# An adaLN transformer block on one core: reordered loads, layer norm and projections around the chunk boundaries

## The chip, the cores and the metric

One core of a Trainium2 chip (trn2) runs the whole program. The metric is device time in microseconds. The kernel before took 952.77 us in the median of five runs (951.03 to 953.43).

## What is computed

A block of 2048 tokens and width 1024, in bf16. Six modulation vectors come from one condition vector; linear attention with 32 heads of 32 is followed by a gated feed-forward network (FFN) of width 3584.

```python
mod = (silu(c) @ w_mod).reshape(1, 6, 1, -1)
sa, ca, ga, sb, cb, gb = (mod[:, i] for i in range(6))
h = layernorm(x) * (1 + ca) + sa
q, k, v = split_heads(h @ wqkv)
pq, pk = phi(q), phi(k)            # phi(t) = where(t > 0, t + 1, exp(t)) + 1e-6
o = (pq @ (pk^T v)) / (pq . sum(pk) + 1e-6)
x = x + ga * (merge_heads(o) @ wo)
h = layernorm(x) * (1 + cb) + sb
x = x + gb * ((gelu(h @ w_gate) * (h @ w_up)) @ w_down)
```

## The kernel before

The program is one list of operations in Python order. A recorder (`T.op`, `T.mm`, `T.dma`) puts each operation into the queue of its engine and adds the semaphore waits that its operands need; so the order in the source is the order on every engine, and an instruction that waits holds up all that stands behind it on the same engine. All matmuls are recorded at L209 and most DMAs at L197. In SBUF one arena is divided by hand, and buffers that lie over each other make waits.

Tokens go in 16 tiles of 128, and in 4 chunks of 512.

*K/V stage.* Four 1 MB panels of w_mod give the vectors ca and sa (`modT_vec`). Then each tile passes the stages of `ln_stages` in a software pipeline (`run_pipeline`): statistics on VectorE, a power on GpSimd (L445), the normalised tile on ScalarE (L451), a DMA transpose on the SP queue (L454), the modulation by eight 128x128 instructions on GpSimd (L460). `kv_groups` multiplies the tile by the panels in the order k0, v0, k1, v1. The four panel loads are one hook (`kv_panel_loads`), ahead of the first transpose on SP.

*Attention.* A loop over `p` takes pairs of tiles: q products, the chain on VectorE that gives the scaled features (`chain_pair`, from `d_prod` at L594 to `d_pqs` at L616), their transposes on SP (L623), the numerator of a chunk (`numT`, evicted by ScalarE at L631), and half an output projection (`wo_proj`, evicted at L644) from a queue. `wo_proj` also issues the loads of the x tiles of the next chunk on GpSimd's queue.

*FFN.* For each chunk, seven pairs of gate and up panels (1 MB each) pass through four panel slots; each pair gives 64 matmuls of 512 columns (448 a chunk), and the GELU runs on ScalarE (L738, L739, L743) and VectorE (L740, L741, L746, the last step of a chunk at L750). Then 224 matmuls make the down projection of the chunk's four tiles; VectorE scales and adds (L771, L775) and GpSimd's queue issues the store.

The input of the FFN, hT2, is made by the second layer norm. For chunk 0 its first six stages are recorded at `p == npairs`, its transposes and modulations behind all output projections. For the later chunks the six stages stand ahead of the down projection, and the transpose and the modulation of tile jj are recorded behind the store of tile jj (`pendingF`). hT2 lies over the last part of oT, which the output projections read. The normalised tiles of chunk 0, hn2a, lie where the first part of the down weights goes.

## Time and profile before

| | us |
|---|---|
| median of five runs | 952.77 |
| lowest, highest | 951.03, 953.43 |
| profiled execution, its own time | 950.31 |
| span of the profiled execution | 948.5 |
| TensorE (PE) busy in it | 854.5 |
| VectorE (DVE) | 442.4 |
| ScalarE (ACT) | 336.7 |
| GpSimd (POOL) | 166.5 |

The profile is of one execution. A busy time is the sum of an engine's instructions; it is an average over stages, so a hole of TensorE has to be read at its place: which wait ended it. Matmul instructions overlap and some of their records can be missing, so counts of matmuls in a stretch can be a few low. PE stands for the matmuls, PEld for their weight loads, SPq for the SP engine's queue of DMA issues.

### The profile page before, as it was taken

The page shows a single profiled execution, that of the slowest core. Times are in us where ns is not written, and L with a number is a line of the kernel's source. Part 1 is how long each engine was busy: PE and PEld are TensorE (multiplying, and loading weights), DVE is VectorE, ACT ScalarE, POOL GpSimd, SP SyncE. Part 2 cuts the span into 40 slices and gives each one's busy share as a digit, 9 for nine tenths or more (in the row PEclk, how much of TensorE's full clock was granted, in tenths as well). Part 3 has the DMA queues.
Part 4 walks back from the last instruction along what each step waited for, and adds up shares of the span by engine and source line. Part 5 has one row for each costly group of instructions (what it writes and reads, how often), then busy time and mean ns, then how long its engine had stood idle before and what let it go on. Part 6 is the DMA issues. An engine that isn't in the chain of part 4 may idle for free.

```text
span 948.5 us, 11061 instructions
## 1 busy us (share of the span) xinstructions
PE 854.5 (90%) x4193; PEld 389.2 (41%) x4193; DVE 442.4 (47%) x890; ACT 336.7 (36%) x572; POOL 166.5 (18%) x352
## 2 busy tenths in 40 slices
PE   1399999999977499989979998979999897999898
PEld 1144445544432144434434443434444343444343
DVE  5165431399873155563135556115555412555411
ACT  1244431465545154441025444004455201544300
POOL 3596632000011400002310000330000231000000
PEclk9999999999997699999989999989999998999999
DMA  9755208334322956707014521702541530534000
GB/s 328 193 150 161 41 16 275 125 67 78 71 53 55 296 178 225 264 3 221 34 40 150 178 88 27 218 23 89 178 138 41 126 130 11 178 125 142 1 23 22
DMA packets 131189, 112.91 MB, mean 119 GB/s; under 512 B 52801, under 2 KB 122433, under 8 KB 131137
## 3 DMA queue, kind: packets, MB, share of 16 engines
q1 hardware_dynamic: 125104, 91.24, 33.3%
q0 software_dynamic: 6016, 20.98, 6.5%
q8 instruction: 33, 0.54, 0.2%
q14 instruction: 20, 0.16, 0.1%
q10 hardware_dynamic: 16, 0.00, 0.0%
HBM read 95.42 MB, written 4.19 MB: 105 GB/s over the span
## 4 chain that ended last, share of the span: by engine, by line
PE 84%; issue 6%; DVE 3%; DMA 2%; ACT 2%; POOL 2%; SPq 0%; POOLq 0%; ACTq 0%; DVEq 0%
PE ps L209 84%; DMA arena<-in_w_mod_dram 2%; POOL arena L460 1%; DVE arena L599 0%; DVE arena L616 0%; ACT arena L631 0%; DVE arena L589 0%; ACT arena L451 0%; DMA arena<-arena 0%; DVE arena L771 0%; ACT arena L644 0%; DVE arena L750 0%; DVE arena L775 0%; ACT arena L739 0%; DVE arena L594 0%
## 5 line engine op out<-in xcount | busy, mean ns | idle before, releaser
L209 PE MATMUL ps<-arena 128*128 128x512 bf16 (+2 forms) x4192 | 854.4, 365 | 83.1 <-POOL arena L460 31.1
L209 PEld LDWEIGHTS ps<-arena 128*128 128x128 bf16 x4192 | 389.1, 99 | 548.0 <-issue 72.0
L738 ACT ACTIVATE arena<-ps 128x512 bf16<-128x512 f32 x112 | 66.9, 597 | 227.6 <-PE ps L209 227.6
L741 DVE SCALAR_TENSOR_TENSOR arena<-ps,arena 128x512 bf16<-128x512 f32 x112 | 77.5, 692 | 120.4 <-ACT arena L739 120.4
L460 POOL TENSOR_SCALAR arena<-arena 128x128 bf16<-128x128 bf16 x256 | 113.9, 456 | 50.1 <-DMA arena<-arena 49.2
L740 DVE SCALAR_TENSOR_TENSOR arena<-arena,ps 128x512 bf16<-128x512 bf16 x112 | 77.1, 688 | 93.0 <-ACT arena L738 93.0
L739 ACT ACTIVATE arena<-ps 128x512 bf16<-128x512 f32 x112 | 66.9, 597 | 130.6 <-PE ps L209 130.6
L771 DVE TENSOR_TENSOR arena<-ps,arena 128x512 bf16<-128x512 f32 x32 | 22.1, 692 | 146.6 <-PE ps L209 146.6
L445 POOL TENSOR_TENSOR arena<-arena 128x1 f32<-128x1 f32 x32 | 18.0, 568 | 344.8 <-DVE arena L442 344.8
L746 DVE SCALAR_TENSOR_TENSOR arena<-arena 128x512 bf16<-128x512 bf16 x108 | 73.6, 682 | 0.0
L743 ACT ACTIVATE arena<-arena 128x512 bf16<-128x512 bf16 x112 | 69.6, 622 | 0.0
L197 POOL DMA_DIRECT2D out_dram<-arena x16 | 9.3, 584 | 245.5 <-DVE arena L775 245.5
L451 ACT ACTIVATE arena<-arena 128x1024 bf16<-128x1024 bf16 x32 | 38.0, 1233 | 27.2 <-DVE arena L448 27.2
L197 POOL DMA_DIRECT2D arena<-in_A_x_dram x32 | 17.9, 562 | 115.5 <-DVE arena L647 77.1
L644 ACT ACTIVATE arena<-ps 128x512 bf16<-128x512 f32 x32 | 18.7, 595 | 33.7 <-PE ps L209 33.7
L578 ACT ACTIVATE arena<-ps 128x512 bf16<-128x512 f32 x32 | 19.5, 609 | 19.4 <-PE ps L209 11.3
L647 DVE TENSOR_TENSOR arena<-arena 128x512 bf16<-128x512 bf16 x32 | 13.2, 424 | 27.0 <-ACT arena L644 26.8
L496 ACT ACTIVATE arena<-ps 128x512 bf16<-128x512 f32 x16 | 9.6, 598 | 37.9 <-PE ps L209 37.9
L494 ACT ACTIVATE arena<-ps 128x512 bf16<-128x512 f32 x16 | 9.6, 598 | 37.7 <-PE ps L209 37.7
L436 DVE BATCH_NORM_STATS2 arena<-arena 128x6 f32<-128x512 bf16 x32 | 21.6, 675 | 0.0
L435 DVE BATCH_NORM_STATS2 arena<-arena 128x6 f32<-128x512 bf16 x32 | 20.7, 647 | 0.0
L579 ACT ACTIVATE arena<-ps 128x512 bf16<-128x512 f32 x32 | 19.5, 608 | 0.0
(49 smaller groups left out, 218.5 us busy)
## 6 DMA issues: line engine op xcount, KB each, us to landing
arena<-in_B_w_gate_dram SPq DMA_DIRECT2D x28, 1024.0 KB, 5.3
arena<-in_B_w_up_dram SPq DMA_DIRECT2D x28, 1024.0 KB, 7.3
arena<-in_A_x_dram POOLq DMA_DIRECT2D x32, 256.0 KB, 3.2
arena<-in_w_mod_dram POOLq DMA_DIRECT2D x8, 1024.0 KB, 12.1
arena<-in_B_w_down_dram SPq DMA_DIRECT2D x7, 1024.0 KB, 9.6
arena<-in_A_wqkv_dram SPq DMA_DIRECT2D x6, 1024.0 KB, 12.4
arena<-in_w_mod_dram SPq DMA_DIRECT2D x4, 1024.0 KB, 14.2
out_dram<-arena POOLq DMA_DIRECT2D x16, 256.0 KB, 2.3
```

The costliest lines, as they stand in the source:

```text
L197: return self.op(eng, lambda e: e.dma_start(out_ap, in_ap), R=R, W=W, ctr=ctr, inc=16)
L209: ins = t.matmul(o, l, r, start=(fs and i == 0), stop=(ls and i == n - 1))
L436: T.op("dve", lambda v: v.bn_stats(st[:, 6:12], x_ap[:, 512:1024]), R=[x_ap], W=[st[:, 6:12]])
L451: T.op("act", lambda a: a.activation(hn, x_ap, AF.Identity, bias=nm, scale=rs), R=[x_ap, nm, rs], W=[hn])
L460: T.op("pool", lambda g, blk=blk, t=t: g.tensor_scalar(blk, blk, c1T[:, t:t + 1], sT[:, t:t + 1], ALU.mult, ALU.add), R=[blk, c1T, sT], W= ...
L738: T.op("act", lambda a, sqz=sqz, bg=bg: a.activation(sqz, bank(bg), AF.Square, scale=math.sqrt(GELU_A)), R=[bank(bg)], W=[sqz])
L739: T.op("act", lambda a, usb=usb, bu=bu: a.activation(usb, bank(bu), AF.Copy), R=[bank(bu)], W=[usb])
L740: T.op("dve", lambda v, sqz=sqz, bg=bg: v.scalar_tensor_tensor(sqz, sqz, 1.0, bank(bg), ALU.add, ALU.mult), R=[sqz, bank(bg)], W=[sqz])
L741: T.op("dve", lambda v, dstA=dstA, usb=usb, bg=bg: v.scalar_tensor_tensor(dstA, bank(bg), 0.5, usb, ALU.mult, ALU.mult), R=[bank(bg), usb] ...
L743: T.op("act", lambda a, th=th, sqz=sqz: a.activation(th, sqz, AF.Tanh, scale=GELU_C), R=[sqz], W=[th])
L746: T.op("dve", lambda v, pd=pd, pth=pth: v.scalar_tensor_tensor(pd, pth, 1.0, pd, ALU.add, ALU.mult), R=[pth, pd], W=[pd])
L771: T.op("dve", lambda v, dst=dst, b=b, cols=cols: v.tensor_tensor(dst, bank(b), modGB[:, cols], ALU.mult), R=[bank(b), modGB[:, cols]], W=[ ...
```

## The change

1. The K/V panels are loaded in two hooks: k0 and v0 first, k1 and v1 at step 6 of the pipeline, which is behind the first transpose. The slots follow the order k0, v0, k1, v1.
2. `modT_vec` gets a parameter to hand back its eviction instead of issuing it. Both calls leave it off, so the order there is the old one. `load_panel` and `wd_part` get a parameter for the queue, which nobody uses.
3. Chunk 0's second layer norm writes a buffer of its own, hT2a, at 8 KB of the arena, where only the broadcast vector bc of the K/V stage had been. The chain of the last pair of tiles moves into `p == 7`. In `p == 7` the output projection stands behind the transposes and the numerator, and numerator 2 so ahead of half of projection 1. The layer norm's first five stages are recorded at `p == 8`, the normalising on ScalarE between the last tiles of projection 2, then the transposes; tiles 0 and 1 are modulated on GpSimd, tiles 2 and 3 on ScalarE between the tiles of projection 3.
4. The first gate and up panels are loaded at `p == 8`, ahead of the transposes of tiles 14 and 15. The first panel of chunk 0 is a call of its own (`gateup_panel`, the old loop body). The first part of the down weights is loaded at panel 2.
5. For the later chunks, the whole layer norm with transposes and modulations is recorded ahead of the down projection and its stores.
6. The first down product of a chunk is two groups of matmuls on the same bank, 26 and 2 of the 28 tiles of AT, each with its own waits.

```diff
-    def load_panel(src_ap):
+    def load_panel(src_ap, eng="sp"):
...
-        T.dma("sp", panel[k], src_ap, d_panel[k])
+        T.dma(eng, panel[k], src_ap, d_panel[k])
...
+    hT2a = view(8 * KB, [P, 4, NDT, P], BF16)
...
+    ks0, vs0, ks1, vs1 = [(panel_use[0] + i_) % NPANEL for i_ in range(4)]
 
     def kv_panel_loads():
-        a = [load_panel(wqkv_v[:, :, n * 512:(n + 1) * 512]) for n in (2, 3, 4, 5)]
-        assert tuple(a) == (ks0, ks1, vs0, vs1)
+        a = [load_panel(wqkv_v[:, :, n * 512:(n + 1) * 512]) for n in (2, 4)]
+        assert a == [ks0, vs0]
+
+    def kv_panel_loads_2():
+        a = [load_panel(wqkv_v[:, :, n * 512:(n + 1) * 512]) for n in (3, 5)]
+        assert a == [ks1, vs1]
...
     add_hook(1, kv_panel_loads)
+    add_hook(6, kv_panel_loads_2)
...
+    def ln2_0_items():
+        return [ln_stages(x1[:, jj, :], cb1T, sbT, hT2a[:, jj, :, :], d_trh[jj], hn2a_t, mod_eng=("pool" if jj < 2 else "act")) for jj in range(4)]
...
-        if 1 <= p <= npairs:
+        if 1 <= p < npairs:
             chain_pair(2 * (p - 1), 2 * (p - 1) + 1)
         if er_a is not None:
             q_minadd(er_a)
             q_minadd(er_b)
             q_ttadd(er_a)
             q_ttadd(er_b)
-        if wo_queue:
+            if p == npairs - 1:
+                chain_pair(2 * p, 2 * p + 1)
+        if p == npairs:
+            its0 = ln2_0_items()
+            run_pipeline([st_[:5] for st_ in its0])
+        if p < 7 and wo_queue:
             q_, jjs = wo_queue.pop(0)
             wo_proj(q_, jjs)
...
+        if 7 <= p <= npairs and wo_queue:
+            q_, jjs = wo_queue.pop(0)
+            wo_proj(q_, jjs)
         if p == npairs:
-            ln2_0_build()
-            run_pipeline([st_[:6] for st_ in ln2_0_items])
-    while wo_queue:
-        q_, jjs = wo_queue.pop(0)
-        wo_proj(q_, jjs)
-    for st_ in ln2_0_items:
-        st_[6]()
-    for st_ in ln2_0_items:
-        st_[7]()
+            kg0 = load_panel(wg_v[:, :, 0:512])
+            ku0 = load_panel(wu_v[:, :, 0:512])
+        if p == npairs + 1:
+            wo_queue.pop(0)
+            wo_proj(2, (2,))
+            its0[0][5]()
+            its0[1][5]()
+            wo_proj(2, (3,))
+            its0[2][5]()
+            its0[3][5]()
+            for st_ in its0:
+                st_[6]()
+            its0[0][7]()
+            its0[1][7]()
+    wo_proj(3, (0, 1))
+    its0[2][7]()
+    wo_proj(3, (2,))
+    its0[3][7]()
+    wo_proj(3, (3,))
...
+    gateup_panel(0, 0, hT2a, kg0, ku0)
     for q in range(NSC):
-        prevA = None
+        hT2c = hT2a if q == 0 else hT2
         for n in range(NFP):
+            if q == 0 and n == 0:
+                continue
...
+            if q == 0 and n == 2:
+                wd_part(0)
...
         if q + 1 < NSC:
-            nxt = ln2_items(q + 1)
-            run_pipeline([st_[:6] for st_ in nxt])
-            pendingF = [(st_[6], st_[7]) for st_ in nxt]
-        else:
-            pendingF = []
+            run_pipeline(ln2_items(q + 1))
...
-                T.mm(its)
+                if jj == 0 and dc == 0:
+                    T.mm(its[:26], last_stop=False)
+                    T.mm(its[26:], first_start=False)
+                else:
+                    T.mm(its)
...
-            if pendingF:
-                ftr, fmod = pendingF.pop(0)
-                ftr()
-                fmod()
```

Three places show how the instructions now stand; lines of the changed kernel have other numbers. First SP's queue at the start of the program, as a piece of the difference (all buffers lie in the arena; a transpose of L454 is L458 in the changed kernel):

```order
 L197 DMA arena<-in_w_mod_dram 128x8x512 x4
-L197 DMA arena<-in_A_wqkv_dram 128x8x512 x4
-L454 DMA_TRANSPOSE arena<-arena 128x8x128 x16
+L197 DMA arena<-in_A_wqkv_dram 128x8x512 x2
+L458 DMA_TRANSPOSE arena<-arena 128x8x128
+L197 DMA arena<-in_A_wqkv_dram 128x8x512 x2
+L458 DMA_TRANSPOSE arena<-arena 128x8x128 x15
```

The first transpose stands behind two panel loads instead of four, the others behind four loads and the first transpose.

Second ScalarE's queue at the end of the attention part, from the last q product to the first instruction of the FFN. Before (L631 evicts a numerator, L644 an output projection, L451 normalises, L738 is the FFN):

```order
L579 ACTIVATE arena<-ps 128x512
L644 ACTIVATE arena<-ps 128x512 x4
L631 ACTIVATE arena<-ps 128x512 x8
L644 ACTIVATE arena<-ps 128x512 x4
L451 ACTIVATE arena<-arena 128x1024 x4
L644 ACTIVATE arena<-ps 128x512 x4
L631 ACTIVATE arena<-ps 128x512 x8
L644 ACTIVATE arena<-ps 128x512 x8
L738 ACTIVATE arena<-ps 128x512
```

The same stretch of ScalarE's queue in the changed kernel (L636 for L631, L649 for L644, L455 for L451, L688 for L738, and L467 modulates):

```order
L584 ACTIVATE arena<-ps 128x512
L636 ACTIVATE arena<-ps 128x512 x8
L649 ACTIVATE arena<-ps 128x512 x8
L636 ACTIVATE arena<-ps 128x512 x8
L649 ACTIVATE arena<-ps 128x512 x2
L455 ACTIVATE arena<-arena 128x1024 x2
L649 ACTIVATE arena<-ps 128x512 x2
L455 ACTIVATE arena<-arena 128x1024 x2
L649 ACTIVATE arena<-ps 128x512 x4
L467 ACTIVATE arena<-arena 128x128 x8
L649 ACTIVATE arena<-ps 128x512 x2
L467 ACTIVATE arena<-arena 128x128 x8
```

Numerator 2 moved ahead of half of projection 1, the normalising went from ahead of projection 2's second half and numerator 3 to between its last two tiles, and two modulations of eight instructions came in between the tiles of projection 3.

Third GpSimd's queue at the boundary from chunk 0 to chunk 1 of the FFN, before (L445 is the power of the layer norm, L460 the modulation):

```order
L445 TENSOR_TENSOR arena<-arena 128x1 x4
L197 DMA out_dram<-arena 128x1024
L460 TENSOR_SCALAR arena<-arena 128x128 x8
L197 DMA out_dram<-arena 128x1024
L460 TENSOR_SCALAR arena<-arena 128x128 x8
L197 DMA out_dram<-arena 128x1024
L460 TENSOR_SCALAR arena<-arena 128x128 x8
L197 DMA out_dram<-arena 128x1024
L460 TENSOR_SCALAR arena<-arena 128x128 x8
```

The same boundary of GpSimd's queue in the changed kernel (L449 for L445, L464 for L460):

```order
L449 TENSOR_TENSOR arena<-arena 128x1 x4
L464 TENSOR_SCALAR arena<-arena 128x128 x32
L197 DMA out_dram<-arena 128x1024 x4
```

All four modulations stand ahead of the four stores.

## Rows read from the trace of the kernel before

**Rows 1.** Page, part 1: busy us (share of the span) and instructions of each engine.

```profile
PE 854.5 (90%) x4193; PEld 389.2 (41%) x4193; DVE 442.4 (47%) x890; ACT 336.7 (36%) x572; POOL 166.5 (18%) x352
```

**Rows 2.** Waits of PE: line, awaited engine: us in total, times, longest.

```profile
PE ps L209 <- POOL arena L460: 31.1, 2, 17.2
PE ps L209 <- issue: 18.5, 3, 6.4
PE ps L209 <- DVE arena L750: 10.5, 4, 2.6
```

**Rows 3.** Timeline, PE, 255 to 345: start, us, instructions, idle before and releaser.

```profile
254.78 10.09 PE L209 MATMUL ps<-arena 128*128 128x512 bf16 x46
267.75 14.85 PE L209 MATMUL ps<-arena 128*128 128x512 bf16 x68 [2.88 <-ACT arena L631]
287.23 2.06 PE L209 MATMUL ps<-arena 128*128 128x512 bf16 x4 [4.63 <-ACT arena L644]
292.58 16.28 PE L209 MATMUL ps<-arena 128*128 128x512 bf16 x64 [3.29 <-ACT arena L631]
322.73 22.59 PE L209 MATMUL ps<-arena 128*128 128x512 bf16 x92 [13.87 <-POOL arena L460]
```

**Rows 4.** Windows: us, busy us of PE, PEld, DVE, ACT, POOL, PEclk, DMA share, GB/s.

```profile
322.73:328.00 5.27, 5.27 (x13) 1.87 (x14) 0.69 (x1) 0.60 (x1) 0.00 (x0) 0.50 1.09 353
479.64:482.00 2.36, 2.36 (x6) 0.84 (x7) 0.00 (x0) 0.00 (x0) 0.00 (x0) 0.50 0.00 0
550.00:570.00 20.00, 20.00 (x94) 9.11 (x93) 11.15 (x17) 10.08 (x18) 0.00 (x0) 1.00 0.33 106
```

**Rows 5.** Chain that ended last, in order of time: start, us, work; FFN stages.

```profile
322.73 99.44 PE ps L209 x448
...
424.77 48.53 PE ps L209 x224
...
793.20 99.72 PE ps L209 x448
```

**Rows 6.** Timeline, DVE: first and last step of the chain of tiles 14 and 15.

```profile
264.82 1.29 DVE L594 TENSOR_TENSOR arena<-arena 128x1024 bf16<-128x1024 bf16 x2
...
269.18 2.35 DVE L616 TENSOR_TENSOR arena<-arena 128x1024 bf16<-128x1024 bf16 x2
```

**Rows 7.** DMA issues: queue, count, KB each, median us to landing (whole span; 18 to 40).

```profile
arena<-in_B_w_up_dram SPq DMA_DIRECT2D x28, 1024.0 KB, 7.3
...
arena<-in_A_wqkv_dram SPq DMA_DIRECT2D x2, 1024.0 KB, 12.7
```

**Rows 8.** Lines of ACT, forms apart: count, busy us, mean ns, idle before.

```profile
L451 ACT ACTIVATE arena<-arena 128x1024 bf16<-128x1024 bf16 x32 | 38.0, 1233 | 27.2 <-DVE arena L448 27.2
...
L644 ACT ACTIVATE arena<-ps 128x512 bf16<-128x512 f32 x32 | 18.7, 595 | 33.7 <-PE ps L209 33.7
...
L404 ACT ACTIVATE arena<-ps 128x8 f32<-128x8 f32 x2 | 0.4, 178 | 23.8 <-PE ps L209 23.8
```

**Rows 9.** Timeline, boundary from chunk 0 to 1: transposes, last store, last modulation.

```profile
431.44 5.39 SPq L454 DMA_TRANSPOSE arena<-arena  x4
...
475.24 0.59 POOL L197 DMA_DIRECT2D out_dram<-arena  x1 [8.00 <-DVE arena L775]
475.88 3.44 POOL L460 TENSOR_SCALAR arena<-arena 128x128 bf16<-128x128 bf16 x8
```

**Rows 10.** Timeline and chain, K/V start; a load, the first transpose, what follows.

```profile
15.42 4.87 SPq L197 DMA_DIRECT2D arena<-in_A_wqkv_dram  x2
...
24.52 6.48 SPq L454 DMA_TRANSPOSE arena<-arena  x1
...
35.05 3.44 POOL L460 TENSOR_SCALAR arena<-arena 128x128 bf16<-128x128 bf16 x8 [11.19 <-DMA arena<-arena]
...
38.60 134.41 PE ps L209 x824
...
48.72 0.60 ACT L494 ACTIVATE arena<-ps 128x512 bf16<-128x512 f32 x1 [1.24 <-PE ps L209]
```

More of the change, by code (lines that the diff above doesn't have):

```diff
@@ L394, in _build, with modT_vec @@
     T.op("pool", lambda g: g.iota(vm.rearrange("p (a b) -> p a b", a=4), [[DH, 4], [0, DH]], base=0, channel_multiplier=-1), W=[vm])
-    def modT_vec(pan_lo, pan_hi, dstT, plus1, b):
+    def modT_vec(pan_lo, pan_hi, dstT, plus1, b, defer=False):
         for t in range(NDT):
@@ L403, in modT_vec @@
         if plus1:
-            T.op("act", lambda a: a.activation(dstT, src, AF.Identity, bias=1.0, scale=1.0), R=[src], W=[dstT])
+            ev = lambda: T.op("act", lambda a: a.activation(dstT, src, AF.Identity, bias=1.0, scale=1.0), R=[src], W=[dstT])
         else:
-            T.op("act", lambda a: a.activation(dstT, src, AF.Copy), R=[src], W=[dstT])
-    modT_vec(panel[pan_ca0], panel[pan_ca1], ca1T, True, next_bank())
-    modT_vec(panel[pan_sa0], panel[pan_sa1], saT, False, next_bank())
+            ev = lambda: T.op("act", lambda a: a.activation(dstT, src, AF.Copy), R=[src], W=[dstT])
+        if defer:
+            return ev
+        ev()
+    early_mod_evacs = [modT_vec(panel[pan_ca0], panel[pan_ca1], ca1T, True, next_bank()),
+                       modT_vec(panel[pan_sa0], panel[pan_sa1], saT, False, next_bank())]
     T.op("dve", lambda v: v.tensor_scalar(t1m, vm, 0.0, None, ALU.is_le), R=[vm], W=[t1m])
@@ L660, in chain_pair, with gateup_panel, gelu_flush @@
                 f(t_)
-    ln2_0_items = []
-    def ln2_0_build():
-        for jj in range(4):
-            ln2_0_items.append(ln_stages(x1[:, jj, :], cb1T, sbT, hT2[:, jj, :, :], d_trh[jj], hn2a_t))
+    def ln2_0_items():
+        return [ln_stages(x1[:, jj, :], cb1T, sbT, hT2a[:, jj, :, :], d_trh[jj], hn2a_t, mod_eng=("pool" if jj < 2 else "act")) for jj in range(4)]
+    gelu_cnt = [0]
+    gelu_state = {"prevA": None}
+    def gateup_panel(q, n, hT2c, kg, ku):
+        for j4 in range(4):
+            jf = n * 4 + j4
+            kk = gelu_cnt[0]
+            gelu_cnt[0] += 1
+            bg = next_bank()
+            bu = next_bank()
+            items_g = [(bank(bg), panel[kg][:, t, j4 * P:(j4 + 1) * P], hT2c[:, :, t, :]) for t in range(NDT)]
+            items_u = [(bank(bu), panel[ku][:, t, j4 * P:(j4 + 1) * P], hT2c[:, :, t, :]) for t in range(NDT)]
+            T.mm(items_g)
+            T.mm(items_u)
+            sqz = sqz_t[kk % NGT]
+            th = th_t[kk % NGT]
+            usb = usb_t[kk % NGT]
+            dstA = AT[:, jf, :]
+            T.op("act", lambda a, sqz=sqz, bg=bg: a.activation(sqz, bank(bg), AF.Square, scale=math.sqrt(GELU_A)), R=[bank(bg)], W=[sqz])
+            T.op("act", lambda a, usb=usb, bu=bu: a.activation(usb, bank(bu), AF.Copy), R=[bank(bu)], W=[usb])
+            T.op("dve", lambda v, sqz=sqz, bg=bg: v.scalar_tensor_tensor(sqz, sqz, 1.0, bank(bg), ALU.add, ALU.mult), R=[sqz, bank(bg)], W=[sqz])
+            T.op("dve", lambda v, dstA=dstA, usb=usb, bg=bg: v.scalar_tensor_tensor(dstA, bank(bg), 0.5, usb, ALU.mult, ALU.mult),
+                 R=[bank(bg), usb], W=[dstA])
+            T.op("act", lambda a, th=th, sqz=sqz: a.activation(th, sqz, AF.Tanh, scale=GELU_C), R=[sqz], W=[th])
+            if gelu_state["prevA"] is not None:
+                pd, pth = gelu_state["prevA"]
+                T.op("dve", lambda v, pd=pd, pth=pth: v.scalar_tensor_tensor(pd, pth, 1.0, pd, ALU.add, ALU.mult),
+                     R=[pth, pd], W=[pd])
+            gelu_state["prevA"] = (dstA, th)
+    def gelu_flush():
+        if gelu_state["prevA"] is not None:
+            pd, pth = gelu_state["prevA"]
+            T.op("dve", lambda v, pd=pd, pth=pth: v.scalar_tensor_tensor(pd, pth, 1.0, pd, ALU.add, ALU.mult), R=[pth, pd], W=[pd])
+            gelu_state["prevA"] = None
     npairs = NST // 2
@@ L723, in _build @@
                 wd_part(n)
[L724 to L757 removed]
+            if q == 0 and n == 2:
+                wd_part(0)
+            gateup_panel(q, n, hT2c, kg, ku)
+        gelu_flush()
+        if q + 1 < NSC:
+            run_pipeline(ln2_items(q + 1))
         for jj in range(4):
@@ L777, in _build @@
             T.dma("pool", out2d[j * P:(j + 1) * P, :], stg, d_o[so % NXR])
-            if pendingF:
-                ftr, fmod = pendingF.pop(0)
-                ftr()
-                fmod()
-        while pendingF:
-            ftr, fmod = pendingF.pop(0)
-            ftr()
-            fmod()
     for k in range(NXR):
```

38 lines of the change are left out of this document (2 added, 36 removed).

## The prediction

> **What bounds the kernel now.** I began with the page's busy line: TensorE is busy for 854.5 of 948.5 us, 90%, and no other engine is near that [rows 1]. So the kernel is a chain of matmuls with holes, and the questions are which work ends each hole late and what the matmuls just behind a hole cost. The list of TensorE's waits names the big holes [rows 2]: two on the GpSimd line that applies the modulation (31.1 us, 17.2 and 13.9), three of some 6.2 us put down to "issue" (18.5 us), four on the last GELU step on VectorE (10.5 us). The timeline of TensorE around the end of the attention part [rows 3] shows four more close together: 2.88, 4.63, 3.29 and 13.87 us. The windows [rows 4] show what follows a long hole: from 322.73 and from 479.64 the granted clock is 0.50, the 1.2 GHz level, with matmuls half as fast, while in the middle of a panel it is 1.00, the 2.4 GHz level. After the 2.6 us hole ahead of the down projection nothing is lost: 224 matmuls in 48.53 us are 216.6 ns each [rows 5]. I use that as the full-speed price of one 512-column matmul.
>
> **The change part by part.**
>
> *Second layer norm of the first chunk (chunk 0).* Before, its transposes write hT2, which lies over the tail of oT, so they wait until the last output projection has read oT; then come three tiles of modulation on GpSimd, and only then the first gate matmul, at 322.73. The numerator product of chunk 2 ends at 254.78 + 10.09 = 264.87 [rows 3]. From there to 322.73 there are 136 matmuls, 29.5 us at 216.6 ns: without holes or half speed the gate would start at 294.3. The difference, 28.4 us, is what can be had; in it are the holes 2.88 + 4.63 + 3.29 + 13.87 = 24.7 and the slow pieces of [rows 3] (64 matmuls in 16.28 us where 13.9 would do). The new order leaves the same number of matmuls: numerator 2 moves ahead of 32 of them (half of output projection 1).
>
> Is everything else ready by 294.3? I lay the new order on that clock, counting back: output projection 3 takes 6.93 + 3.47 + 3.47, so its parts end at 287.4, 290.8 and 294.3; projection 2's last two tiles end at 277.0 and 280.5; numerator 3 starts at 271.8.
> (a) The attention chain of tiles 14 and 15 on VectorE ran from 264.82 to 271.53, 6.7 us [rows 6]. It now stands ahead of half of projection 1 and starts some 5 us earlier, near 260, so its two transposes are issued by 267. On SP they stand behind two new 1 MB panel loads; these may start when the last q product has run, near 257, and a load of that kind lands 7.3 us after its issue [rows 7], so they are out of the way by 266. The transposes land about 270, 2 us before numerator 3 needs them. This is the tightest place on SP.
> (b) ScalarE normalises tiles 0 and 1 behind the eviction that ends at 277.6, at 1.23 us each [rows 8], then tiles 2 and 3 behind the one at 281.1; the last transpose is issued near 283.6 and lands by 287. GpSimd modulates tiles 0 and 1 in 2 x 3.45 us [rows 9] after its last x load, near 284 to 291: in time.
> (c) Tiles 2 and 3 are now modulated on ScalarE, 8 instructions of 128x128 each, which the trace does not show. The nearest rows are 178 ns for 8 columns and 595 ns for 512 [rows 8]; by columns between them 128 columns take 0.28 us, so a tile 2.2 us. Tile 2: 288.0 to 290.2; the two evictions of the next projection tile to 291.9; tile 3 to 294.1. Just in time: stall 0. At 0.18 us it is earlier still; at 0.60 us a tile is 4.8 us, tile 3 ends near 298.7, and the stall is 4.4 us. I take 0, the value by columns.
> The Trainium skill's page "ScalarE: Activation LUTs", section "What ACT_TABLE_LOAD costs", speaks against this part: it gives an instruction a fixed cost, and more for each per-partition scale or bias, of which these have both. By its figures I estimate 0.39 us each, back to back; tile 3 would end near 295.3 and the gate would wait 1.0 us, so the sum would be 1.0 us smaller. No run here shows it yet.
> (d) TensorE hands eight banks to ScalarE at numerator 2 and again at 3: I allow 0.5 us. Term: 28.4 - 0.5 = **27.9 us**, from 22 (the 4.4 us stall, and a short slow restart) to 28.4.
> (e) The first gate and up panels are loaded early. The second pair needs the slots of the output weights, free only at 294.3; 7.3 us to landing and a load in front of it make some 9 to 10 us, and the first panel's 64 matmuls cover 13.9. Cost nothing; without that cover, up to 3 us. The first down weights move two panels later, with 27 us of matmuls in front.
>
> *Chunk boundaries.* After each of the first three down projections, the last output store waits on GpSimd for VectorE, and the last tile's modulation stands behind it in the queue: 475.24, then 475.88 for 3.44 us [rows 9], and the gate starts at 479.64. Now all four modulations stand ahead of the stores. The transposes are issued between 431.44 and 436.8 [rows 9], so four times 3.45 us end near 452, with 21 us of down projection left; the stores, which nobody waits for but the ring, start some 10 us later. The hole goes, three times. Term: **18.5 us** [rows 2], bounded by 3 x 6.4 = 19.2.
>
> *Split of the first down product.* It read all 28 tiles of AT at its first matmul and so waited for the last GELU step. Now the first 26 wait for nothing late: 26 x 0.2166 = 5.6 us of cover for a tail of 2.6 us. Term: **10.5 us** over four chunks [rows 2].
>
> *Clock.* The gate/up stages take 99.44 to 99.72 us for 448 matmuls [rows 5], where 448 x 0.2166 = 97.05: 2.4 to 2.7 us each, and [rows 4] put that into the first 5 us behind the hole. With the holes gone it goes too, four times: **10.1 us**; 0 is the other bound.
>
> *K/V start.* The first transpose was issued at 24.52, behind four 1 MB loads, and GpSimd's modulation waited for it until 35.05 [rows 10]. Now it stands behind two. The second of these was issued at 15.42 and lands 12.7 us later [rows 7, 10], near 28.1; the transpose then needs about 1.35 us (four were issued in 5.39 us [rows 9]): 29.5, modulation to 33.0, where 38.60 is the first K matmul now. The group of tile 0 takes 8.4 us (38.60 to the second group, 48.72 - 1.73 = 47.0 [rows 10]), so it ends at 41.4. Tile 1's transpose now follows all four loads and one transpose: 35.0 + 1.35, modulated by 39.9, ahead of 41.4. Behind that TensorE runs without holes to 173, at four groups of 1.73 us a tile against 3.45 us of modulation and some small work on GpSimd, so the shift is kept. Term: 41.4 against 47.0, **5.6 us**; bounds 0 (the transpose doesn't get ahead) and 8.4 (the group wholly hidden). A loss is excluded: the last load is put back by one transpose to about 35.5 and isn't needed before 39.
>
> *The deferral of the early evictions* is off by default, and both are still issued in place: nothing.
>
> **Sum.** 27.9 + 18.5 + 10.5 + 10.1 + 5.6 = 72.6 us. The profiled execution took 950.31 us (span 948.5), so it would be 877.7. The median of the five runs is 952.77, 2.5 us above the profiled one; with that the forecast is **880 us**.
>
> **The rivals.**
> 1. *The layer norm of chunk 0 is still late.* ScalarE's modulation at 0.60 us, or the transposes of tiles 14 and 15 landing behind the panels. For it: slack of 0 to 2 us in (a) and (c). Against: GpSimd and SP have 3 us or more elsewhere. Price 4.4 + 2.5 for a slow restart: **887 us**. Chance 0.13.
> 2. *The K/V start gains nothing*, because the transpose still shares its way with the loads. For it: in [rows 10] its issue alone took 6.48 us. Against: the two loads ahead of it are nearly done by then. 5.6 us less: **886 us**. Chance 0.12.
> 3. *The change doesn't do what it says at the boundaries*: the holes stay because something else is late by the same time, say the down product's tail after all (10.5) and half the clock term (5). **896 us**. Against: every cover above is over twice what it hides. Chance 0.08.
> 4. *Slower than before*, by one mechanism: TensorE, without its pauses, isn't granted the full level in the FFN. The FFN has 4 x (97.05 + 48.53) = 582 us of full-speed matmuls; the gain of 72.6 is used up where the mean granted clock there falls to 582/(582 + 72.6) = 0.89, and at 0.85 the time would be about **983 us**. Against: 1.00 was granted from 550 to 570 [rows 4] with TensorE busy all along, and the half level only behind holes. Chance 0.02.
>
> **How the numbers follow.** The forecast has 0.65. All terms at their good bounds (28.4, 19.2, 10.5, 10.1, 8.4) give 876; below that I leave 3 us for what the medians vary. On the other side rivals 1 and 2 together are some 892 to 893, and rival 3 begins beyond. The range is 873 to 895. It leaves out rivals 3 and 4 and part of the clock's bound, under 2 in 10. About 0.2% can be told from no change here; all cases but rival 4 are far on one side: faster 0.97, same 0.01, slower 0.02.
>
> **What would show it.** In the profile after: the first gate matmul near 288 (294.3 less the shift of 5.6), with no hole over 1 us in the 35 us before it; the second K/V group near 41; the 128x128 instruction on ScalarE near 0.28 us; no wait on the GELU tail; gate/up stages of 97 us following the down stages without a hole, at a granted clock of 1.00. Wrong would be a wait on ScalarE's modulation or on a panel load in front of a gate product, a first modulation on GpSimd still at 35, or a clock below 1.00 where TensorE is busy.

## The result and the profile after

The changed kernel took 879.9 us in the median of nine runs (877.99 to 885.54), beside 953.31 us in the median of fifteen runs of the kernel before. The ratio is 0.9238, with a 95% interval of 0.9222 to 0.9254. The span of the profiled execution went from 948.5 to 877.8 us; its own time is 879.9.

The page of the changed kernel, from parts 1 and 2 (the busy line answers to [rows 1]; PEclk is the clock granted to TensorE, each digit a fortieth of the span in tenths, 9 for 90% and more):

```profile
PE 840.3 (96%) x4193; PEld 386.4 (44%) x4193; DVE 442.6 (50%) x890; ACT 342.1 (39%) x588; POOL 163.9 (19%) x336
...
PEclk9999999999999999999999999999999999999999
```

TensorE was busy for 854.5 us and now for 840.3: the work is the same, so 14 us of the 70.7 us of span were slower matmuls, nearly all of them at the lower level of the clock. The other 56 us were holes. The waits of TensorE in the changed kernel (line, awaited engine, us in total, times, longest), to be laid beside [rows 2] (L464 is the modulation on GpSimd, L467 the one on ScalarE):

```profile
PE ps L209 <- POOL arena L464: 12.3, 1, 12.3
...
PE ps L209 <- DMA arena<-arena: 2.3, 2, 1.8
...
PE ps L209 <- ACT arena L467: 0.9, 1, 0.9
```

The waits on "issue" (18.5 us) and on the last GELU step (10.5 us) are gone from the list. Of the two on GpSimd one is left, at the K/V start. The timeline of TensorE shows the same in order of time (start, us, instructions, idle before and its releaser), beside [rows 3]:

```profile
33.74 165.23 PE L209 MATMUL ps<-arena 128*128 128x512 bf16 x960 [12.32 <-POOL arena L464]
...
201.28 66.39 PE L209 MATMUL ps<-arena 128*128 128x512 bf16 x305 [0.17 <-ACT arena L584]
269.49 22.61 PE L209 MATMUL ps<-arena 128*128 128x512 bf16 x104 [1.82 <-DMA arena<-arena]
292.99 580.33 PE L209 MATMUL ps<-arena 128*128 128x512 bf16 x2688 [0.89 <-ACT arena L467]
```

The whole FFN, 4 x 672 matmuls, is one unbroken piece from 292.99 on, at 580.33 / 2688 = 215.9 ns a matmul. Where the 70.7 us of span went can be read off three marks of TensorE: the start of the q products, the start of the first gate product, and the end. The q products in the timeline before, then in the chain after:

```profile
173.68 29.51 PE L209 MATMUL ps<-arena 128*128 128x512 bf16 x136 [0.69 <-ACT arena L535]
```

```profile
169.46 8.81 PE ps L209 x40
```

| mark | before | after | gain up to here | gain of the part | forecast of the part |
|---|---|---|---|---|---|
| q products begin | 173.68 | 169.46 | 4.2 | K/V start 4.2 | 5.6 |
| first gate product | 322.73 | 292.99 | 29.7 | layer norm of chunk 0: 25.5 | 27.9 |
| end of the span | 948.5 | 877.8 | 70.7 | FFN 41.0 | 18.5 + 10.5 + 10.1 = 39.1 |

### The profile page after: what moved, and what is told of

It reads as the page before. It is cut to its first block, busy times and chain, and to the rows that moved or that the text cites. A ratio compares the mean times of both kernels' runs of the same rounds, so it can differ in the third digit from the quotient of the medians.

```text
span 877.8 us, 11065 instructions
## 1 busy us (share of the span) xinstructions
PE 840.3 (96%) x4193; PEld 386.4 (44%) x4193; DVE 442.6 (50%) x890; ACT 342.1 (39%) x588; POOL 163.9 (19%) x336
## 4 chain that ended last, share of the span: by engine, by line
PE 88%; DVE 4%; issue 3%; DMA 3%; ACT 1%; POOL 1%; SPq 0%; POOLq 0%; ACTq 0%; DVEq 0%
PE ps L209 88%; DMA arena<-in_w_mod_dram 2%; DVE arena L604 1%; DVE arena L621 1%; DMA arena<-arena 1%; ACT arena L467 1%; DVE arena L594 1%; DVE arena L599 1%; POOL arena L464 0%; SPq L197 0%; ACT arena L583 0%; DVE arena L590 0%; DVE arena L612 0%; ACT arena L649 0%; ACT arena L584 0%
## 5 line engine op out<-in xcount | busy, mean ns | idle before, releaser
L209 PE MATMUL ps<-arena 128*128 128x512 bf16 (+2 forms) x4192 | 840.1, 362 | 26.6 <-POOL arena L464 12.3
L688 ACT ACTIVATE arena<-ps 128x512 bf16<-128x512 f32 x112 | 66.9, 597 | 179.5 <-PE ps L209 179.5
L464 POOL TENSOR_SCALAR arena<-arena 128x128 bf16<-128x128 bf16 x240 | 112.3, 481 | 39.4 <-DMA arena<-arena 39.0
L449 POOL TENSOR_TENSOR arena<-arena 128x1 f32<-128x1 f32 x32 | 17.6, 553 | 321.0 <-DVE arena L446 320.1
L455 ACT ACTIVATE arena<-arena 128x1024 bf16<-128x1024 bf16 x32 | 38.1, 1233 | 20.6 <-DVE arena L452 20.6
L649 ACT ACTIVATE arena<-ps 128x512 bf16<-128x512 f32 x32 | 18.9, 603 | 21.7 <-PE ps L209 21.4
```

The lines of the kernel that those rows point to most:

```text
L209: ins = t.matmul(o, l, r, start=(fs and i == 0), stop=(ls and i == n - 1))
L455: T.op("act", lambda a: a.activation(hn, x_ap, AF.Identity, bias=nm, scale=rs), R=[x_ap, nm, rs], W=[hn])
L464: T.op("pool", lambda g, blk=blk, t=t: g.tensor_scalar(blk, blk, c1T[:, t:t + 1], sT[:, t:t + 1], ALU.mult, ALU.add), R=[blk, c1T, sT], W= ...
L688: T.op("act", lambda a, sqz=sqz, bg=bg: a.activation(sqz, bank(bg), AF.Square, scale=math.sqrt(GELU_A)), R=[bank(bg)], W=[sqz])
```

## The experiments

Every kernel is the changed one with the edit shown, except the first. Times are medians; the ratio is to runs of the kernel before that were taken beside it. The changed kernel's are 879.9 and 0.9238.

**The K/V loads alone.** The kernel before with only the loads in two pairs:

```diff
+    ks0, vs0, ks1, vs1 = [(panel_use[0] + i_) % NPANEL for i_ in range(4)]
...
-        a = [load_panel(wqkv_v[:, :, n * 512:(n + 1) * 512]) for n in (2, 3, 4, 5)]
+        a = [load_panel(wqkv_v[:, :, n * 512:(n + 1) * 512]) for n in (2, 4)]
+    def kv_panel_loads_2():
+        a = [load_panel(wqkv_v[:, :, n * 512:(n + 1) * 512]) for n in (3, 5)]
     add_hook(1, kv_panel_loads)
+    add_hook(6, kv_panel_loads_2)
```

> The kernel before with nothing but the K/V panels loaded in two pairs, the second behind the first transpose. Theory (the shift is kept to the end): the first K product starts near 33.7 as in the changed kernel, and the run is 3.6 to 5.6 us shorter than before (about 948 to 949.5 beside 953). Rival (a later stage takes the shift back, a load or a wait that doesn't move with TensorE): under 1 us shorter.

It took 948.02 us, ratio 0.9939 (0.9925 to 0.9954): 4 to 7 us shorter, as the theory has it. Its timeline of TensorE around the second half of the attention part:

```profile
33.83 165.09 PE L209 MATMUL ps<-arena 128*128 128x512 bf16 x960 [12.44 <-POOL arena L460]
...
263.48 16.54 PE L209 MATMUL ps<-arena 128*128 128x512 bf16 x68 [2.88 <-ACT arena L632]
...
320.30 99.54 PE L209 MATMUL ps<-arena 128*128 128x512 bf16 x448 [13.84 <-POOL arena L460]
```

The shift is 4.3 us at 263.48 (267.75 before), but only 2.4 at the first gate product. The 68 matmuls behind the hole of 2.88 us took 16.54 us here and 14.85 before, behind a hole of the same length [rows 3]. A short hole can cost a slow start or none; this comes back below.

**Without the split of the first down product.**

```diff
-                if jj == 0 and dc == 0:
-                    T.mm(its[:26], last_stop=False)
-                    T.mm(its[26:], first_start=False)
-                else:
-                    T.mm(its)
+                T.mm(its)
```

> The changed kernel with the first down product in one piece, waiting for all 28 tiles of AT. Theory (the cover is whole, the split is worth its four holes): four holes of 2.6 us on the last GELU step come back, 10.5 us longer (about 890), and no slow start behind them, since 2.6 us holes cost no clock before. Rival (the earlier modulation has made the boundary tighter, or the hole now lowers the clock): 13 to 20 us longer.

It took 895.69 us, ratio 0.9395 (0.9373 to 0.9416), some 15 us longer than the changed kernel. The rival holds, in its second form: the holes have their old length, and now lower the clock. Timeline of TensorE:

```profile
290.39 96.87 PE L209 MATMUL ps<-arena 128*128 128x512 bf16 x448 [0.89 <-ACT arena L467]
389.87 146.68 PE L209 MATMUL ps<-arena 128*128 128x512 bf16 x672 [2.62 <-DVE arena L703]
539.16 146.90 PE L209 MATMUL ps<-arena 128*128 128x512 bf16 x672 [2.62 <-DVE arena L703]
688.68 146.90 PE L209 MATMUL ps<-arena 128*128 128x512 bf16 x672 [2.62 <-DVE arena L703]
```

The four holes of 2.62 us are back, 10.5 us. But 672 matmuls also take 146.7 to 146.9 us where 672 x 0.2159 = 145.1: 1.6 to 1.8 us more behind three of them, 5.2 us in all. (The FFN of this profile starts 2.6 us earlier than in the changed kernel's, which has a hole of 1.82 us ahead of numerator 3 that is missing here.) The window behind the first hole of this kernel, and then the one behind the same hole of the kernel before (us, busy us of PE, PEld, DVE, ACT, POOL, granted clock, DMA share, GB/s):

```profile
389.87:393.00 3.13, 3.13 (x8) 1.16 (x9) 3.10 (x8) 0.00 (x0) 0.46 (x1) 0.52 0.03 5
```

```profile
424.77:427.77 3.00, 3.00 (x14) 1.38 (x15) 2.97 (x8) 0.00 (x0) 0.33 (x1) 1.00 0.03 5
```

Same wait, same length, the same kind of work around it: 0.52 here (the lower level for nearly all of it), 1.00 there. So the split is worth about 15 us in the new arrangement. In the kernel before its four holes are 10.5 us [rows 2]; no run has the split there by itself.

**The modulations of the later chunks back behind the stores.**

```diff
-            run_pipeline(ln2_items(q + 1))
+            nxt = ln2_items(q + 1)
+            run_pipeline([st_[:6] for st_ in nxt])
+            pendingF = [(st_[6], st_[7]) for st_ in nxt]
...
             T.dma("pool", out2d[j * P:(j + 1) * P, :], stg, d_o[so % NXR])
+            if pendingF:
+                ftr, fmod = pendingF.pop(0)
+                ftr()
+                fmod()
```

> The changed kernel with the transposes and modulations of chunks 1 to 3 put back behind the stores of the down projection. Theory: three holes of 6.2 us on GpSimd's last modulation and three slow starts of 2.5 us come back, 26 us longer (about 906), with gate/up stages of 99.5 us again behind the holes. Rival (the clock term is not due to the holes): 18.5 us longer (about 898) with stages of 97 us.

It took 908.25 us, ratio 0.9514 (0.9485 to 0.9543), 28 us longer. Timeline of TensorE, first chunk boundaries:

```profile
295.47 145.21 PE L209 MATMUL ps<-arena 128*128 128x512 bf16 x672 [0.89 <-ACT arena L467]
447.04 147.51 PE L209 MATMUL ps<-arena 128*128 128x512 bf16 x672 [6.35 <-issue]
600.64 147.51 PE L209 MATMUL ps<-arena 128*128 128x512 bf16 x672 [6.09 <-issue]
```

Holes of 6.35 and 6.09 us (6.12 at the third) and, behind each, a chunk that takes 2.3 us longer than the one without a hole: 18.6 + 6.9 = 25.5, as the theory says. Another 2.5 us arose ahead of the FFN, at a place that the edit doesn't touch: the hole ahead of numerator 3 is 2.23 us here for 1.82, and the 104 matmuls behind it took 24.29 us for 22.61. The rival, by which the slow starts have another cause, falls.

**Chunk 0's layer norm in the old buffer.**

```diff
-        return [ln_stages(x1[:, jj, :], cb1T, sbT, hT2a[:, jj, :, :], d_trh[jj], hn2a_t, mod_eng=("pool" if jj < 2 else "act")) for jj in range(4)]
+        return [ln_stages(x1[:, jj, :], cb1T, sbT, hT2[:, jj, :, :], d_trh[jj], hn2a_t, mod_eng=("pool" if jj < 2 else "act")) for jj in range(4)]
...
             its0[2][5]()
             its0[3][5]()
-            for st_ in its0:
-                st_[6]()
-            its0[0][7]()
-            its0[1][7]()
     wo_proj(3, (0, 1))
-    its0[2][7]()
     wo_proj(3, (2,))
-    its0[3][7]()
     wo_proj(3, (3,))
+    for st_ in its0:
+        st_[6]()
+    for st_ in its0:
+        st_[7]()
...
-    gateup_panel(0, 0, hT2a, kg0, ku0)
+    gateup_panel(0, 0, hT2, kg0, ku0)
     for q in range(NSC):
-        hT2c = hT2a if q == 0 else hT2
+        hT2c = hT2
```

> The changed kernel with chunk 0's layer norm writing the old buffer hT2 again, so that its four transposes and modulations (GpSimd for two tiles, ScalarE for two) stand behind all output projections; the rest of the new order stays. Theory (the buffer of its own carries most of the 25.5 us, the order the rest): a hole of about 12 us ahead of the first gate product plus 2.5 us of slow start, less the 0.9 us wait that is gone: 13 to 14 us longer (about 893.5). Rival (the order alone does it, the buffer little): under 5 us longer. Rival (the buffer alone does it): 25 us longer.

It took 894.36 us, ratio 0.9373 (0.9349 to 0.9398), 13 to 14 us longer, the number of the theory. Timeline and window of TensorE:

```profile
270.37 25.09 PE L209 MATMUL ps<-arena 128*128 128x512 bf16 x104 [4.30 <-DMA arena<-arena]
306.63 23.62 PE L209 MATMUL ps<-arena 128*128 128x512 bf16 x102 [11.17 <-ACT arena L467]
```

```profile
306.63:309.00 2.37, 2.37 (x6) 0.86 (x7) 0.00 (x0) 0.00 (x0) 0.00 (x0) 0.50 1.07 377
```

The first gate product is 13.6 us later than in the changed kernel, and starts at the lower level. But only 10.3 of the 13.6 us are the hole ahead of it (11.17 us for 0.89). At numerator 3, which the edit doesn't touch, 5.0 us more were lost (a hole of 4.30 us for 1.82, and 25.09 us for 22.61 behind it), and TensorE came there 1.6 us earlier. With the slow start behind the gate, which makes the FFN 1.4 us longer, this profile puts the buffer at some 12 us, about half of the 25.5; that the sum of the theory came out so close is in part luck. The rest falls to the new order around numerator 2 and the early normalising, by subtraction: no run takes these away.

**The first gate panels behind the transposes of tiles 14 and 15.**

```diff
-        if p == npairs:
-            kg0 = load_panel(wg_v[:, :, 0:512])
-            ku0 = load_panel(wu_v[:, :, 0:512])
         if p == npairs + 1:
+            kg0 = load_panel(wg_v[:, :, 0:512])
+            ku0 = load_panel(wu_v[:, :, 0:512])
```

> The changed kernel with the first gate and up panel loads moved behind the transposes of tiles 14 and 15 on SP. Theory (the 1.8 us hole ahead of numerator 3 is these two panels, 2 MB, in front of the transposes): the transposes land 3.2 to 4 us after their issue instead of 6.1, the hole goes, 1.8 us shorter (about 878). Rival (the x loads on GpSimd's queue or the pace of VectorE hold them up): hole and time unchanged.

It took 883.89 us, ratio 0.9277 (0.9258 to 0.9295): 4 us longer, against both. Its timeline of TensorE and ScalarE:

```profile
200.23 88.84 PE L209 MATMUL ps<-arena 128*128 128x512 bf16 x409 [0.17 <-ACT arena L584]
295.73 579.57 PE L209 MATMUL ps<-arena 128*128 128x512 bf16 x2673 [6.67 <-ACT arena L467]
```

```profile
288.46 3.18 ACT L467 ACTIVATE arena<-arena 128x128 bf16<-128x128 bf16 x8 [5.67 <-DMA arena<-arena]
```

The hole ahead of numerator 3 is indeed gone, but a larger one stands ahead of the gate: ScalarE waits 5.7 us for a transpose of the layer norm. Those transposes took 9.0 us to land in the median, 4.3 in the changed kernel, although the panels had landed (at 273.24) before the first of them was issued (at 273.58). The theory missed what else is in motion there; the run with the x loads on SP's queue takes this up.

**The first gate panels one step earlier.**

```diff
-        if p == npairs:
+        if p == npairs - 1:
             kg0 = load_panel(wg_v[:, :, 0:512])
             ku0 = load_panel(wu_v[:, :, 0:512])
```

(In the order of the queue: directly behind the transposes of tile 11.)

> The changed kernel with the first gate and up panel loads one step earlier on SP, ahead of the transposes of tiles 12 and 13 and directly behind the last q product. Theory (the hole of up to 1.8 us ahead of numerator 3 is the tail of these 2 MB in front of the last two transposes): the loads start 2.6 us earlier, the transposes of tiles 14 and 15 land in under 4 us, the hole goes, the layer norm's transposes stay free, and the gate starts 1 to 2 us earlier (about 878.5). Rival (the DMA engines are slowed by something else at this place): the hole stays.

It took 879.61 us, ratio 0.9239 (0.9221 to 0.9257): no change. The hole ahead of numerator 3 is gone, and a wait of 3.3 us on ScalarE's modulation has taken its place ahead of the gate. That the panels make the hole stays likely, not shown: the kernel without the split, with the same queue order at this place as the changed one, had no such hole either. Eight of the kernels here have this order, and in their profiles the hole goes with the time to landing of the first panel: with 7.3 to 8.5 us (five kernels) there is a hole of 1.1 to 4.3 us, with 5.4 to 6.2 us (three) there is none. What makes the panels land late is open.

**Tiles 2 and 3 modulated on VectorE.** `ln_stages` gets a branch for VectorE:

```diff
-mod_eng=("pool" if jj < 2 else "act")
+mod_eng=("pool" if jj < 2 else "dve")
...
     its0[2][7]()
-    wo_proj(3, (2,))
     its0[3][7]()
+    wo_proj(3, (2,))
     wo_proj(3, (3,))
```

> The changed kernel with tiles 2 and 3 of chunk 0 modulated on VectorE behind the third and fourth tile's transposes instead of on ScalarE. Theory (16 instructions of 0.4 us each on ScalarE are the 0.9 us wait ahead of the first gate product): the wait goes, 0.9 us shorter (about 879). Rival (GpSimd's two tiles or the evictions are late by as much): the same time, the wait then put down to another engine.

It took 880.49 us, ratio 0.9244 (0.9229 to 0.9259). In the profile the wait of 0.9 us is gone (16 instructions of 0.31 us on VectorE), no other has come, and the span is 876.9. The median can't tell a gain of 0.9 us.

**The early evictions held back.** `defer=True` in both calls, and the hooks:

```diff
-    add_hook(1, kv_panel_loads)
-    add_hook(6, kv_panel_loads_2)
+    add_hook(6, lambda: [ev() for ev in early_mod_evacs])
+    add_hook(6, kv_panel_loads)
+    add_hook(7, kv_panel_loads_2)
```

> The changed kernel with the parameter that holds back the early evictions switched on: they stand on ScalarE behind the first two normalisations, and on SP the first transpose stands ahead of the first pair of K/V loads, the second ahead of the second pair. Theory (the K/V start hangs on the transposes standing behind loads, and the loads themselves are moved at the pace of the DMA engines): the first K product near 25.5 and the second group near 37 instead of 43.4, 6 us shorter (about 874). Rival (the loads, pushed back by the transposes, now end late): the second group after 41, under 2.5 us shorter.

It took 876.74 us, ratio 0.921 (0.9191 to 0.923), about 3 us shorter; half of what was expected. Timeline of TensorE at the K/V start:

```profile
26.68 5.90 PE L209 MATMUL ps<-arena 128*128 128x512 bf16 x16 [5.15 <-POOL arena L464]
33.88 1.90 PE L209 MATMUL ps<-arena 128*128 128x512 bf16 x8 [1.29 <-DMA arena<-in_A_wqkv_dram]
36.99 157.54 PE L209 MATMUL ps<-arena 128*128 128x512 bf16 x936 [1.21 <-DMA arena<-in_A_wqkv_dram]
```

The first product starts 7 us earlier, but now the k1 and v1 panels come late: two holes that end with the landing of a load, and the first group ends at 36.99 + 1.90 = 38.9 where 43.4 was. The start is at the pace of the loads. Further on, 1.1 us of the gain went into a longer wait on ScalarE ahead of the gate (2.0 for 0.9 us).

**Extra matmuls ahead of the K/V stage.**

```diff
+    T.mm([(bank(7), ones, bc[:, 0:4, :]) for _ in range(40)])
     ks0, vs0, ks1, vs1 = [(panel_use[0] + i_) % NPANEL for i_ in range(4)]
```

> The changed kernel with 40 extra matmuls of 512 columns into an unused bank, between the modulation vectors and the first K product, whose result nobody reads. Theory (the first K/V group takes 9.65 us because TensorE starts at its lower level behind a 12 us hole): the extra matmuls end before 33.7, the first group takes 6.9 to 7.5 us, 2.2 to 2.7 us shorter (about 877.5). Rival (the transfers that run at the same time slow it): still 9.6 us, the same time.

It took 878.06 us, ratio 0.9235 (0.9201 to 0.9269), which can't be told from the changed kernel; three of its four runs were 877.0 to 878.5, and the profiled one 884.2. In that one:

```profile
33.13 48.51 PE L209 MATMUL ps<-arena 128*128 128x512 bf16 x224 [0.69 <-issue]
86.09 9.14 PE L209 MATMUL ps<-arena 128*128 128x512 bf16 x31 [4.45 <-POOL arena L465]
```

224 matmuls in 48.51 us are 216.6 ns each from the first one on: the first K/V group takes 7.1 us (its second group begins at 41.96 - 1.73 = 40.23) instead of 9.65. So it is what TensorE did before that made the group slow, as the clock theory says; the transfers, which are the same, do not slow it. But then TensorE stops for 4.45 us, which the changed kernel doesn't: GpSimd had waited for a transpose.

```profile
82.06 3.88 POOL L465 TENSOR_SCALAR arena<-arena 128x128 bf16<-128x128 bf16 x8 [12.79 <-DMA arena<-arena]
```

The changed kernel has this wait too (8.9 us at the same place) and the kernel before (8.2 us), but hides it behind TensorE's backlog. It follows the four loads of 1 MB that GpSimd issues at step 12.

**The same with those loads spread.** The four loads at steps 14, 16, 18 and 20:

```diff
-    add_hook(12, mpanel_round1)
+    for k in range(4):
+        add_hook(14 + 2 * k, (lambda k=k: mpanel_load(k)))
```

> The changed kernel with the 40 extra matmuls ahead of the K/V stage, and with the four loads of the second set of modulation panels on GpSimd's queue spread over four later steps of the pipeline instead of all at step 12. Theory (the 4 MB in one go hold up a transpose for 9 to 13 us, which the earlier K/V stage can no longer hide): GpSimd's wait of 9 to 13 us near 70 shrinks below 4, the 4.5 us hole of TensorE near 82 goes, the gain of 2.4 us from the warm start is whole in every run (about 877). Rival (the wait is the transposes' own pace or the x loads): wait and hole stay.

It took 876.88 us, ratio 0.9207 (0.9191 to 0.9223), 3 us shorter than the changed kernel. The DMA issues from 60 to 80 (queue, count, KB each, median us to landing), first of the changed kernel, then of this one:

```profile
arena<-in_w_mod_dram POOLq DMA_DIRECT2D x4, 1024.0 KB, 10.2
arena<-in_A_x_dram POOLq DMA_DIRECT2D x2, 256.0 KB, 6.0
arena<-arena SPq DMA_TRANSPOSE x3, 8.0
```

```profile
arena<-in_w_mod_dram POOLq DMA_DIRECT2D x1, 1024.0 KB, 5.9
arena<-in_A_x_dram POOLq DMA_DIRECT2D x2, 256.0 KB, 3.9
arena<-arena SPq DMA_TRANSPOSE x3, 3.0
```

A transpose lands in 3.0 us instead of 8.0, GpSimd waits 1.5 us at most instead of 8.9, and the hole is gone.

**The x loads of the last chunk on SP's queue.** The gate panels as in the run above where they stood behind the transposes, `load_x` with a parameter for the queue, and in `wo_proj`:

```diff
-                load_x((q + 1) * 4 + jj, NXR)
+                load_x((q + 1) * 4 + jj, NXR, "sp" if q == 2 else "pool")
```

> The changed kernel with the first gate and up panels behind the transposes of tiles 14 and 15, as in the run where the layer norm's transposes took 9 us to land, and with the four x loads of the last chunk on SP's queue ahead of those transposes instead of on GpSimd's queue. Theory (the transposes are slow there because the x loads of another queue are moved at the same time): the transposes land in under 6 us, ScalarE's modulation no longer waits 5.7 us for one, TensorE's wait ahead of the first gate product is under 1.5 us instead of 6.7, and the run is 3 to 5 us shorter than that one (878 to 881 beside 883.9). Rival (the panels themselves or the transposes' own pace): the wait stays at 5 us or more, about 884.

It took 879.43 us, ratio 0.9238 (0.9223 to 0.9254), 4.5 us shorter than the run it builds on. The issues from 270 to 290:

```profile
arena<-in_A_x_dram SPq DMA_DIRECT2D x4, 256.0 KB, 2.8
...
arena<-arena SPq DMA_TRANSPOSE x4, 4.1
```

The transposes land in 4.1 us instead of 9.0 although they now stand behind 1 MB in their own queue, and TensorE's wait ahead of the gate falls from 6.7 to 2.7 us (not below 1.5 as expected: the first transpose is issued 4 us later). So in that arrangement it was the x loads, in motion at the same time from another queue. They don't always cost as much: the run without the split and the one with the spread loads issue the first x load the same 0.8 us ahead of the first of these transposes, move the same bytes, and there the transposes landed in 4.9 and 4.6 us in the median. What makes the mixture slow in one kernel and not in another stays open. The Trainium skill has a rule that bears on it: "DMA: Bandwidth & Descriptors", section "Queues, rings and completion order", says that each DMA engine takes turns, packet by packet, between the queues that have work for it. The runs fit it (a transpose took 9.0 us beside another queue's loads and 4.1 without them here, 8.0 and 3.0 above), but none shows the turns themselves, and the rule alone doesn't explain 4.6 and 9.0 at the same overlap.

**All together.** The held-back evictions, the spread loads, the gate panels one step earlier, and VectorE's modulation:

> All that the runs point to on top of the changed kernel: the early evictions held back and the transposes ahead of the K/V loads, the second set of modulation panels spread, the first gate panels directly behind the last q product, tiles 2 and 3 of chunk 0 modulated on VectorE. Theory (the gains stand in different holes and add up): 4 us at the K/V start, 1 to 2 us at numerator 3, 1 to 2 us ahead of the first gate product: 6 to 8 us shorter than the changed kernel (about 873). Rival (each takes away the cover of the next): no better than the deferral alone, about 876.5.

It took 872.46 us (871.97 to 872.75), ratio 0.9162 (0.9149 to 0.9174): 7.4 us shorter than the changed kernel, and faster than every other. The timeline of TensorE:

```profile
37.05 157.56 PE L209 MATMUL ps<-arena 128*128 128x512 bf16 x922 [1.17 <-DMA arena<-in_A_wqkv_dram]
195.06 1.67 PE L209 MATMUL ps<-arena 128*128 128x512 bf16 x7 [0.46 <-DMA arena<-arena]
...
197.61 668.28 PE L209 MATMUL ps<-arena 128*128 128x512 bf16 x3067 [0.33 <-ACT arena L641]
```

From 197.61 to the end TensorE has no hole at all. The gains stand in different holes, as the theory has it: of the 7.5 us of span, 4.4 lie ahead of 195.06 (199.44 in the changed kernel), and 2.7 are the holes of 1.82 and 0.89 us. Taken alone, two of the four edits had no gain that the median shows.

## Why the prediction was right, point by point

The forecast was 880 and the median is 879.9. That closeness flatters it: the sum of 72.6 us was 1.9 too large against the span's 70.7, and the 2.5 us that I added from the profiled execution to the median were there before but not after, where the profiled execution has the median's own time. The two errors cancel. And two of the signs that the prediction named as wrong did show, if small: a wait on ScalarE's modulation in front of the first gate product (0.89 us), and a hole over 1 us in the 35 us before it (1.82).

*Layer norm of chunk 0, 27.9 forecast, 25.5 measured.* The mechanism held: without any hole the gate would have started at 294.3 less the shift of 4.2, that is 290.1; it started at 292.99, and waits of 1.82 and 0.89 us are nearly all of the 2.9 between. Step (c) was mis-sized: ScalarE's 128x128 modulation, taken as 0.28 us by columns, is

```profile
L467 ACT ACTIVATE arena<-arena 128x128 bf16<-128x128 bf16 x16 | 6.4, 486 | 0.0
```

486 ns, and eight of them 3.17 us, 0.40 each back to back. So the gate waited 0.89 us where I took 0. From the Trainium skill's figures ("ScalarE: Activation LUTs", section "What ACT_TABLE_LOAD costs") the prediction had estimated 0.39 us and a wait of 1.0: the trace agrees with that, at 0.40 and 0.89. The interpolation by columns failed because both of its rows are of instructions without per-partition operands. Step (a) named the tightest place and was 1.8 us short: the last transpose of tiles 14 and 15 landed 6.1 us after its issue instead of 3. The DMA issues from 255 to 270, and the transposes from 250 to 275:

```profile
arena<-in_B_w_up_dram SPq DMA_DIRECT2D x1, 1024.0 KB, 10.3
```

```profile
DMA to landing us min/median/max: 3.2/5.2/6.1
```

The second panel took 10.3 us to land where step (a) had 7.3, and was still in motion when the transposes were issued. What mixes with a transpose in the DMA engines wasn't in the sum.

*Chunk boundaries, split and clock, 39.1 forecast, 41.0 measured.* All seven holes are gone, and with them the slow starts. The 1.9 us between are the full-speed price, which was a little high: 215.9 ns over 2688 matmuls, not 216.6. The price of one part depends on the others: without the later modulations 25.5 us come back at their place (forecast 18.5 + 7.7), but without the split 15 (forecast 10.5), because in the new arrangement its short holes cost clock.

*K/V start, 5.6 forecast, 4.2 measured (3.6 at the second group).* The first transpose got ahead of the second pair of loads as forecast; modulation began at 30.20 and the first K product at 33.74, for 33.0 in the working. That 0.7 us is the transpose: 1.35 us was the pace at which four are issued, and this one landed 2.4 us behind the load ahead of it. The rest, 1.25 us, is the slow start, which I had carried over as part of a group of 8.4 us. The last 0.6 us of the 4.2 is a short wait ahead of the q products (0.69 us before) that is gone. Timeline of GpSimd and ScalarE in the changed kernel:

```profile
30.20 3.44 POOL L464 TENSOR_SCALAR arena<-arena 128x128 bf16<-128x128 bf16 x8 [6.26 <-DMA arena<-arena]
```

```profile
45.12 0.60 ACT L498 ACTIVATE arena<-ps 128x512 bf16<-128x512 f32 x1 [1.24 <-PE ps L209]
```

The second group starts at 45.12 - 1.73 = 43.4, so the first took 9.65 us. The trace shows why it is longer than before: here the first 13 matmuls start 427 ns apart, there the first 7, and all others 216. The extra matmuls bring the group to 7.1 us, which shows that the pause ahead of it is the cause.

*The rivals.* The first came true in part (0.9 and 1.8 us of its 6.9). The second fell: the loads alone give 4 to 7 us. The third fell: none of the holes at the boundaries is left. The fourth, a lower level in the FFN, fell: TensorE was granted 1.00 while it was busy without pause for 580 us.

*Open.* Why a hole of 2.2 to 3.3 us sometimes costs a slow start and sometimes not is not settled by these runs. Nor is the spread of the changed kernel's own runs (878 to 885.5); that it is the mixing of transposes and loads is only argued, from profiles whose waits differ at places that no edit touched, and from the 0.8 us spread of the combined kernel.

## What to carry to other kernels

Read which instruction ended each hole of the bounding engine, and look in that instruction's queue for work that nobody waits for: a store, an early load, a shared buffer. Here a buffer of 8 KB per partition, a store behind a modulation instead of ahead of it, and a product that waits for what it needs, not for all it reads, gave most of 70 us, beside the new order of loads and projections, with no matmul less. Count the slow start behind a hole with the hole, and expect the holes that stay to grow dearer or to show the next late thing.

## What the runs showed of the hardware

- Holes of TensorE of 2.62 and 2.88 us cost nothing at some places (224 matmuls in 48.53 us, 68 in 14.85) and 1.6 to 1.9 us at others with the same work (672 in 146.9 us where 145.1 is full speed, 68 in 16.54 where 14.7 is). One of 2.23 us cost 1.7 (104 in 24.29 us for 22.61). Holes of 6.1 to 6.4 us cost 2.3 to 2.8 us each time (672 in 147.51 us for 145.21; before, 448 in 99.48 to 99.71 us, which took 96.87 behind a hole of 0.89).
- At the very first dense matmuls the recorded clock doesn't show the slow start. In the changed kernel the window

```profile
33.74:35.24 1.50, 1.50 (x4) 1.00 1.14 346
```

reads 1.00 (columns here: us, busy us of PE, clock, DMA share, GB/s), while four matmuls start in 1.5 us where seven would at full speed; with matmuls ahead of it the same group runs at 216.6 ns each. The first clock record of this trace is the rise to the upper level, at 38.92 us, where the distance of the starts falls from 427 to 216 ns; with the extra matmuls it is at 25.89, ahead of the first K product. Before the first record the column has nothing but its 1.00: there the distance between starts tells, not the clock column.
- A DMA transpose of a 128x1024 tile landed in 3.0 us in the median of three where the loads were spread, and in 8.0 beside four 1 MB loads of another queue. Beside four loads of 256 KB the median of four was 4.3 us in the changed kernel, 4.6 to 4.9 in two others and 9.0 in one.
